# Second LayerNorm of two chunks as a scaling of kept, turned rows, instead of a second turning

## The chip, the cores and the metric

The kernel runs on one core of a Trainium2 chip. The metric is the device time of one execution in microseconds (us). The core has a matrix engine (PE, with its weight loads listed apart as PEld), a vector engine (DVE), a scalar engine (ACT) and GpSimd (POOL); SyncE (SP) issues most DMAs. Each engine works through its own list of instructions in order and waits on semaphores for the others.

## The reference

The input x has 2048 rows of 448 numbers. The kernel computes multi-query attention with 16 heads of width 28 (one head of keys and values for all), and an MLP of width 1792 with a LayerNorm of its own, both on the same normalised rows:

```
xn = layernorm(x)
q = xn @ wq;  k = xn @ wk;  v = xn @ wv
attention = softmax(q k^T / sqrt(28)) v @ wo
y = layernorm(xn)                       # the second LayerNorm
mlp = gelu(y @ w1 + b1) @ w2 + b2
out = x + attention + mlp
```

LayerNorm has no learned scale or shift here. So xn has mean 0, and y is xn times one number for each row: y = a * xn with a = 1 / sqrt(var(xn) + eps).

## The kernel before, in words

The order of the work is written by hand: the kernel states the order of the instructions on each engine, and generators hand out single steps. The 2048 rows are 16 tiles of 128, in four chunks of four tiles (512 rows).

**Precision.** Matrix products that must be exact to float32 are made of three products of halves: each operand is split into a high part (`xh`, rounded to the PE's fp32r type by a copy on ACT) and a low part (`xl`, what is left, by a subtraction on DVE or POOL).

**Turning.** A projection needs the rows with the features on the partitions. `norm_parts` gives two steps for each tile: `center(k)` normalises the tile into `xn` (448 columns on ACT, a last piece of 64 on DVE), and `turn(k)` makes four PE transposes of 128x128 into one PSUM bank, copies the bank to `xh` on ACT (L273) and subtracts `xh` from it on DVE into `xl` (L274). `xh` and `xl` have two buffers each.

**Front** (0 to 67.5 us). For each chunk c there are four slots `q_slot(c, 0..3)`, each a projection of 512 columns by 128 outputs (11 matmuls); their results are evacuated one slot later, by ACT copies and DVE subtractions into `qe`, and stored by SP's queue to DRAM (`qd`), from where the attention loads them by head. Beside chunk c, the next chunk's rows are centered and turned. The fourth chunk has no next one; beside it the first chunk is turned for the second LayerNorm (`second=True`). The strips of w1 are split in the same slots (`w1_split`: ACT copy, two POOL subtractions). `later(c, i, job, ahead)` hangs extra jobs on a slot; `norm_both`, which works out the combined scale `lnq` and shift `lnqb` of both LayerNorms for all 16 tiles, hangs on slots (2, 2) and (2, 3).

**MLP** (67.5 to 475 us). 56 slots: four chunks by 14 strips of 128 hidden units. A slot has the 11 matmuls of the first product (`mlp1`), the 12 of the second (`mlp2`) two slots later, and nine steps for attention in between: row maxima of scores (`max_stream`, L521 and L522) or "turned" scores (`turned_scores`, L555 and L556), which put a fourth head's scores aside in DRAM. The GELU runs on ACT (L603, L604, L609, L616) and POOL (L605, L606, L610, L611, L618). Splitting w2 takes ACT, DVE and POOL in the odd slots of the first 14 (`w2_split`). The chunks go in order 1, 2, 3, 4. In five slots of a chunk (positions 5, 7, 9, 11, 13) `norm_gen` centers and turns a tile of the next chunk for its second LayerNorm; x is loaded again for this by `line(t)`. The first four scores of the MLP and the PSUM tiles of the maxima share one pool of three banks.

**Attention** (475 us to the end). In each step PE makes scores and maxima for one pair of key tiles, ACT takes the exponential, and PE weighs the values. Here the DMAs of the heads are issued by POOL (software DMA), which before are issued by SP.

**Queues.** SP's queue issues in order. A DMA that needs another's data, or a buffer, waits at the head and holds all that stand behind it.

The rows that a chunk needs for its second product are taken in one line of the code before:

```
yh, yl = xts[c, True]
```

Of the kernel before, what the change touches and what calls it, by code (L numbers as in the profile page):

```python
# [9 lines left out]
F32 = mybir.dt.float32  # L10
# [6 lines left out]
P = 128  # L17
# [14 lines left out]
RAWS = 2  # L32
GELU = 0.044715, 0.7978845608028654
LEAD = 11
NH = 8
HD = D // 2

# [2 lines left out]
def block_kernel(ctx, tc, x, wq, wk, wv, wo, w1, b1, w2, b2, out):  # L40
# [20 lines left out]
    ld = dram.tile([4, CW], F32, name="ld")  # L61
    ad = dram.tile([P, NT, D], F32, name="ad")
    td = {u: dram.tile([32, 4, 4 * CT, 512], F32, name=f"td{u}") for u in TURNED}
    qd = [dram.tile([D, S], F32, name=f"qd{i}") for i in range(2)]

    ks = keep.tile([P, S], F32R, name="ks")
# [14 lines left out]
    w1h = wp.tile([P, 4, F], F32R, name="w1h")  # L81
    w1l = wp.tile([P, 3, F], F32R, name="w1l")
    tmp = ph1.enter_context(tc.tile_pool(name="tmp", bufs=2))

    hrp = ph1.enter_context(tc.tile_pool(name="hrp", bufs=3))

# [144 lines left out]
    def norm_both():  # L231
        dve.tensor_mul(lnq, lnp[:, :, 1], lnr)
        dve.tensor_mul(lnq, lnq, lnr)
        r = rstd(lnq, lnq, NT)
        next(r)
        yield
        next(r)
        dve.tensor_mul(lnq, lnq, lnr)
        dve.scalar_tensor_tensor(lnqb, lnp[:, :, 0], -1.0, lnq, op0=ALU.mult, op1=ALU.mult)
        act.activation(warm, one, AF.Tanh)  # L240
        yield

    lines = {}
# [5 lines left out]
    def norm_parts(c, second, first=False, bank=mtile):  # L249
        xh = xt_p.tile([P, 4, CW], F32R, name="xh")  # L250
        xl = xl_p.tile([P, 4, CW], F32R, name="xl")
        xts[c, second] = xh, xl
        xns = {}

        def center(k):
            t = CT * c + k
            if first:
                xn = f(wqp.tile([P, 2, CW], F32R, name="qe", bufs=5))[:, 0, :]
            else:
                xn = tmp.tile([P, 4 * P], F32, name="xn", bufs=2)  # L260
            scale, bias = (lnq, lnqb) if second else (lnr, lnb)
            src = lines.pop(t) if second and c else xin[t]
            act.activation(xn[:, 0:D], src, AF.Identity, bias=bias[:, t:t + 1], scale=scale[:, t:t + 1])
            dve.tensor_scalar(xn[:, D:512], src[:, 384:448], scale[:, t:t + 1], bias[:, t:t + 1],
                              op0=ALU.mult, op1=ALU.add)
            xns[k] = xn

        def turn(k):
            sl = slice(k * P, (k + 1) * P)
            pt = bank([P, 4, P])  # L270
            for b in range(4):
                pe.transpose(pt[:, b, :], xns[k][:, b * P:(b + 1) * P], ident)  # L272
            act.activation(xh[:, :, sl], pt, AF.Copy)  # L273
            dve.tensor_sub(xl[:, :, sl], pt, f(xh[:, :, sl]))  # L274

        return center, turn
# [26 lines left out]
    def norm_gen(c, bank):  # L303
        center, turn = norm_parts(c, True, False, bank)
        for k in range(CT + 1):
            if k > 0:
                turn(k - 1)
            yield
            if k < CT:
                center(k)  # L310
            yield

    wl_q = []

# [98 lines left out]
        for k in range(2):  # L413
            later(c - 1, 0, lambda g=g: next(g), True)
    g = norm_both()
    for k in (2, 3):
        later(2, k, lambda g=g: next(g))

    def b1_turn():
        pb = mtile([P, NF])  # L420
# [23 lines left out]
    turns = itertools.count()  # L444
    evac, vt = None, None
    for c in range(NCH):
        center, turn = norm_parts((c + 1) % NCH, c + 1 == NCH, bank=lambda shape: (qbank, mtile)[next(turns) % 2](shape))
        for i in range(4):
            ev = q_slot(c, i)
            if vt is not None:  # L450
                v_slot(c, vt)
                vt = None
            if evac is not None:
                vt = evac()
            evac = ev
            if i in ((2, 3) if c == 0 else (1, 3)):
                n = 2 * c + i // 3
                w1_split(n)
                if n < 2:
                    w1_load(n + 4)  # L460
                elif n == 3:
                    w1_load2(6)
                elif n in (4, 5):
                    w2_load(n - 4)
                if n in (2, 3):
                    qms.append(load_m(*heads[n - 2]))
                elif n in (4, 5):
                    load_m(TURNED[n - 4], 3, q3[n - 4])
            for job in more.get((c, i, True), ()):
                job()  # L470
            for part, k in (("", "c0 c1", "t0 c2 t1 c3", "t2 t3") if c == 0 else
                            ("c0 c1", "t0 c2 t1 c3", "t2 t3", ""))[i].split():
                (center if part == "c" else turn)(int(k))
            for job in more.get((c, i, False), ()):
                job()
    evac()
    ph1a.close()

    def load_q(u, blocks=range(4)):
# [114 lines left out]
        return c == 0 and ft % 2 == 1  # L594

    def mlp1(c, ft):
        yh, yl = xts[c, True]
        ph = m2p.tile([P, CW], F32, name="m2_3") if (c, ft) == (0, 1) else php.tile([P, CW], F32, name="ph")
        fs = slice(ft * P, (ft + 1) * P)
        yield from proj_steps(ph, lambda b: w1h[:, b, fs], lambda b: w1l[:, b, fs], yh, yl)  # L600
        hx = hrp.tile([P, CW], F32, name="hx", bufs=2)
        hz = hrp.tile([P, CW], F32, name="hz", bufs=2)
        act.activation(hx, ph, AF.Identity, bias=b1t[:, ft:ft + 1])  # L603
        act.activation(hz, ph, AF.Square, bias=b1s[:, ft:ft + 1], scale=GELU[0] ** 0.5)  # L604
        pool.tensor_scalar(hz, hz, 1.0, 1.0, op0=ALU.mult, op1=ALU.add)  # L605
        pool.tensor_mul(hz, hz, hx)  # L606

        def middle():
            act.activation(hz, hz, AF.Tanh, scale=GELU[1])  # L609
            pool.tensor_scalar(hz, hz, 0.5, 0.5, op0=ALU.mult, op1=ALU.add)  # L610
            pool.tensor_mul(hx, hx, hz)  # L611

        def ending():
            hh = hrp.tile([P, CW], F32R, name="hh")
            hl = hrp.tile([P, CW], F32R, name="hl")
            act.activation(hh, hx, AF.Copy)  # L616
            hs[c, ft] = (hh, hl)
            pool.tensor_sub(hl, hx, f(hh))  # L618

        return middle, ending  # L620

    def mlp2(c, ft, stages):
        if ft == 0:
            m2s[c] = [m2p.tile([P, CW], F32, name=f"m2_{k}")[:, 0:D] for k in range(CT)]
        m2 = m2s[c]
        hh, hl = hs.pop((c, ft))
        terms = ((hh, w2h), (hh, w2l), (hl, w2h))
        order = [(k, i) for k in range(CT) for i in range(3)]
        if (c, ft) == (0, 0):
            order.sort(key=lambda e: e[1])  # L630
        for n, (k, i) in enumerate(order):
            h, w = terms[i]
            pe.matmul(m2[k], h[:, k * P:(k + 1) * P], w[:, ft, :], start=(ft == 0 and i == 0),  # L633
                      stop=(ft == NF - 1 and i == 2))
            if ft == NF - 1 and i == 2:
                t = CT * c + k
                a = lines.pop(t)
                dve.tensor_add(a, a, m2[k])
                nc.sync.dma_start(ad[:, t, :], a)
            stages[n]()  # L640
            yield

    def slot(n):
        nonlocal maxed, ending, later_low
        middle = high = low = none
        closing, ending = ending, none
        if n < len(mslots):
            if split(*mslots[n]):
                high, low = w2_split(n // 2)
# [10 lines left out]
            stages, later_low = {0: closing, 1: high, 5: middle}, low  # L660
        if n in norms:
            stages = {4: norms[n], 5: texp, 6: texp, 7: closing, 8: norms[n], 9: middle, 10: low}
        if n >= 2:
            yield from mlp2(*mslots[n - 2], [stages.get(i, none) for i in range(12)])
        else:
            for i in sorted(stages):
                stages[i]()
# [3 lines left out]

    norms, maxed, ending, later_low = {}, 0, none, none
    mslots = [(c, ft) for c in range(NCH) for ft in range(NF)]
    for c in range(1, NCH):
        g = norm_gen(c, lambda shape: php.tile(shape, F32, name="ph"))
        for i in range(CT + 1):
            norms[NF * (c - 1) + 5 + 2 * i] = lambda g=g: next(g, None)
    mxs.add(max_stream())
    done = 0
    for n in range(len(mslots) + 2):  # L680
        c, ft = mslots[n] if n < len(mslots) else (NCH, n - len(mslots))
        if 3 <= ft < 11 and ft % 2 and c < NCH - 1:
            line(CT * (c + 1) + (ft - 3) // 2)
        if 9 < ft:
            line(CT * c + ft - 10)
            if ft > 10:
                a = lines[CT * c + ft - 11]
                pool.tensor_add(a, a, b2b)
        if ft == 0 and n:
            a = lines[CT * c - 1]  # L690
            pool.tensor_add(a, a, b2b)
        if (c, ft) == (NCH - 1, 8):
            load_q(0)
        if (c, ft) == (NCH - 1, 11):
            load_max(0)
        ts = 0
        for _ in slot(n):
            done += 1
            if n >= len(mslots) and done % 3 == 1:
                maxed += mxs.step()  # L700
            elif n < len(mslots) and done * MLP_MAX // 46 > (done - 1) * MLP_MAX // 46:
                if ts < 4 and n < len(mslots) - 1 and not split(c, ft):
                    ts += tq.step()
# [270 lines left out]
```

## Time and profile before

| | us |
|---|---|
| median of 3 runs | 1090.36 (1090.21 to 1091.38) |
| profiled execution | 1091.39 |
| its span in the trace | 1089.6 |
| PE busy | 1077.5 |
| DVE busy | 910.3 |
| ACT busy | 736.8 |
| POOL busy | 561.6 |

The page tells how long each engine was busy in the span, the chain of waits that ended last followed back from the end, and the costliest groups of instructions. The trace also answers for a stretch of time, a line of the code or a tile. A line such as "L618" is a line of the kernel before. The clock that PE was granted was 0.999 of full speed over the span. The last lines of an answer on a tile give the time from a DMA's issue to its landing.

### The profile page before, as it was taken

The numbers are of one execution on the slowest core, as the hardware profiler recorded it, in microseconds if no ns is written. First come the engines' busy times: TensorE is split into PE (matmuls) and PEld (weight loads), VectorE is DVE, ScalarE is ACT, GpSimd is POOL, SyncE is SP. The second block draws the span as 40 slices with busy tenths as digits, with TensorE's granted clock in tenths as the row PEclk, the third lists the DMA queues.
The fourth block names the chain that finished last, engine by engine and source line by source line (L and its number), as shares of the span: only waits on it lengthen the run. The fifth ranks groups of instructions, "written<-read, shape, count | busy, mean of one in ns | idle before, by whom it ended". The sixth has DMA issues, their size and how long they took to land.

```text
span 1089.6 us, 17728 instructions
## 1 busy us (share of the span) xinstructions
PE 1077.5 (99%) x5905; PEld 721.6 (66%) x5905; DVE 910.3 (84%) x1847; ACT 736.8 (68%) x1279; POOL 561.6 (52%) x694
## 2 busy tenths in 40 slices
PE   9999999999999999999999999999999999999998
PEld 8778888888888888865555555555556555455455
DVE  6789889888988998876999997899997889886744
ACT  6775655676666666658777776577775777765784
POOL 5359787768777877864234433433442344243220
PEclk9999999999999999999999999999999999999999
DMA  8774555777877777767987798588796778895720
GB/s 265 221 233 137 154 133 155 193 179 194 211 176 186 187 199 169 219 166 156 197 190 175 184 224 215 131 199 191 182 211 174 176 175 202 193 205 128 189 53 35
DMA packets 140512, 195.16 MB, mean 179 GB/s; under 512 B 17086, under 2 KB 96116, under 8 KB 140420
## 3 DMA queue, kind: packets, MB, share of 16 engines
q1 hardware_dynamic: 127684, 172.11, 63.1%
q0 software_dynamic: 11328, 21.33, 8.7%
q8 instruction: 47, 0.77, 0.3%
q10 hardware_dynamic: 1408, 0.57, 0.2%
q14 instruction: 45, 0.37, 0.1%
HBM read 115.22 MB, written 77.71 MB: 177 GB/s over the span
## 4 chain that ended last, share of the span: by engine, by line
PE 89%; DVE 4%; DMA 3%; ACT 2%; issue 1%; POOL 1%; SPq 0%; DVEq 0%; ACTq 0%; POOLq 0%
PE po L863 20%; PE m L521 18%; PE m L891 17%; PE m L633 11%; PE ph L180 10%; PE m L555 5%; PE m L753 1%; PE m L754 1%; PE m L755 1%; PE ph L185 1%; PE ph L183 1%; PE po L846 1%; DVE xl L274 1%; PE ph L272 1%; DVE mx L522 1%
## 5 line engine op out<-in xcount | busy, mean ns | idle before, releaser
L522 DVE TENSOR_REDUCE mx<-m 128x1 f32<-128x512 f32 x784 | 506.8, 679 | 77.9 <-PE m L521 68.6
L892 ACT ACTIVATE p<-m 128x512 f32<-128x512 f32 x784 | 402.6, 609 | 161.3 <-PE m L891 161.2
L521 PE MATMUL m<-ks,qm 128*128 128x512 f32 x784 | 321.6, 411 | 0.7 <-DVE mx L522 0.6
L891 PE MATMUL m<-xh,ks 128*128 128x512 f32 x784 | 257.2, 397 | 0.1
L863 PE MATMUL po<-p,vs 128*32 128x512 f32 x1920 | 230.8, 598 | 0.0
L521 PEld LDWEIGHTS m<-ks,qm 128*128 128x128 f32 x784 | 147.0, 188 | 117.0 <-ACT p L892 37.0
L891 PEld LDWEIGHTS m<-xh,ks 128*128 128x128 f32 x784 | 146.1, 188 | 42.1 <-issue 5.8
L556 DVE TENSOR_SCALAR_CACHE_REDUCE raw<-m 128x512 f32<-128x512 f32 x240 | 160.9, 689 | 15.3 <-PE m L555 8.6
L874 DVE STREAM_TRANSPOSE p<-half 128x1024 f32<-128x1024 f32 x120 | 148.3, 1236 | 5.3 <-PE m L846 2.0
L573 ACT ACTIVATE raw<-raw,m 128x1024 f32<-128x1024 f32 x120 | 133.0, 1151 | 0.0
L603 ACT ACTIVATE hx<-ph,b1t 128x512 f32<-128x512 f32 x55 | 37.9, 689 | 131.9 <-PE ph L185 124.5
L863 PEld LDWEIGHTS po<-p,vs 128*32 128x32 f32 x1920 | 50.1, 109 | 113.4 <-issue 108.4
L555 PE MATMUL m<-ks,q 128*128 128x512 f32 x240 | 94.8, 395 | 0.9 <-DVE mx L522 0.6
L618 POOL TENSOR_TENSOR hl<-hx,hh 128x512 fp32r<-128x512 f32 x56 | 73.0, 1303 | 35.0 <-ACT hh L616 35.0
L633 PE MATMUL m<-w2h,hl 128*128 128x448 f32 x224 | 82.6, 370 | 1.4 <-POOL hl L618 1.4
L633 PE MATMUL m<-w2l,hh 128*128 128x448 f32 x224 | 81.5, 365 | 0.5 <-DVE w2l L346 0.5
L633 PE MATMUL m<-w2h,hh 128*128 128x448 f32 x224 | 81.4, 364 | 0.0
L611 POOL TENSOR_TENSOR hx<-hx,hz 128x512 f32<-128x512 f32 x56 | 73.0, 1303 | 4.7
L606 POOL TENSOR_TENSOR hz<-hz,hx 128x512 f32<-128x512 f32 x56 | 72.6, 1296 | 4.7
L508 POOL DMA_DIRECT2D xh<-mn x15 | 8.1, 543 | 129.4 <-ACT mn L504 129.3
L180 PE MATMUL ph<-xh,w1h 128*128 128x512 f32 x165 | 65.0, 394 | 0.0
L180 PE MATMUL ph<-xh,w1l 128*128 128x512 f32 x165 | 64.6, 391 | 0.0
(187 smaller groups left out, 1402.3 us busy)
## 6 DMA issues: line engine op xcount, KB each, us to landing
td<-raw SPq DMA_DIRECT2D x240, 256.0 KB
half<-td SPq DMA_DIRECT2D x120, 512.0 KB
xh<-qd POOLq DMA_DIRECT2D x60, 168.0 KB, 4.5
a<-in_A_x_dram SPq DMA_DIRECT2D x32, 224.0 KB
qm<-qd POOLq DMA_DIRECT2D x112, 56.0 KB, 4.3
qd<-qe SPq DMA_DIRECT2D x24, 256.0 KB
qm<-qd SPq DMA_DIRECT2D x84, 56.0 KB
ad<-a SPq DMA_DIRECT2D x16, 224.0 KB
```

The source lines that it names most:

```text
L180: pe.matmul(ps, w, v, start=(n == 0), stop=False)
L521: pe.matmul(pm, qm[:, t * P:(t + 1) * P], ks[:, n * CW:(n + 1) * CW], start=True, stop=True)
L522: dve.tensor_reduce(mx[:, CT * j + t, n:n + 1], pm, axis=AX.X, op=ALU.max)
L555: pe.matmul(sc, q3[i][:, t * P:(t + 1) * P], ks[:, n * CW:(n + 1) * CW], start=True, stop=True)
L556: dve.tensor_scalar(raw[:, :, 4 * n:4 * n + 4, :].rearrange("p r b i -> p b r i"), sc.rearrange("p (b r i) -> p b r i", r=4, i=32), SCALE, ...
L573: act.activation(raw[:, rs], raw[:, rs], AF.Exp, bias=m3[:, 4:5], scale=1.0)
L611: pool.tensor_mul(hx, hx, hz)
L633: pe.matmul(m2[k], h[:, k * P:(k + 1) * P], w[:, ft, :], start=(ft == 0 and i == 0), stop=(ft == NF - 1 and i == 2))
L863: pe.matmul(po[32 * j:32 * j + 32, :], vs[:, kt, :], ps.pop((u, kt, j)), start=(kt == 0), stop=(kt == NT - 1))
L874: dve.transpose(p.rearrange("p k (g j) -> p g k j", j=32), halves[u, kt // 8][:, :, 32 * (kt % 8):32 * (kt % 8) + 64].rearrange("p g (k j) ...
L891: pe.matmul(s, ks[:, kt * P:(kt + 1) * P], qss[u][:, j, :], start=True, stop=True)
L892: act.activation(p, s, AF.Exp, scale=SCALE)
```

## The change

In the front, the rows of chunks 3 and 4 are turned once, for the first LayerNorm, as all chunks are. The change keeps their `xh` and `xl` and scales them in place for the second: row by row by the number a, which for turned rows lies along the free axis.

- `norm_both` moves from slots (2, 2) and (2, 3) to slot (2, 0), and writes the scales a of all tiles to a tile `lna` of its own.
- `scale_rows`, ahead of the turns of slot (2, 1): PE transposes `lna`, DVE copies it, SP stores it to DRAM (`sd`).
- `scale_load`, ahead in slot (2, 2): SP loads a chunk's 512 scales, the same for all partitions, into `ab` (one buffer), chunk 3 first; chunk 4's follow in slot (3, 3).
- For each of the four blocks of features: `join` (DVE adds `xh` and `xl`), `scale` (POOL multiplies by `ab`), `high_part` (ACT copies to `xh`), `low_part` (DVE subtracts to `xl`). For chunk 3 this goes through slots (2, 3) to (3, 2); for chunk 4 through MLP slots 3 to 10, one block in two slots.
- The MLP takes the chunks in the order 3, 4, 1, 2 (`MLP_ORDER`). Only chunks 1 and 2 are turned a second time, beside the second and third position. The front's turning of chunk 1, and its four turns for one chunk in the MLP, are gone, with the loads of four lines of x.
- In MLP slots 3 to 10 one maximum step is left out of each; attention takes those eight.
- The load of the tanh table moves to a job of slot (2, 3).
- `dynamic_dma_scratch_size` is 8192 in place of 16384.

The diff, cut to its core:

```diff
+MLP_ORDER = 2, 3, 0, 1
...
+    sd = dram.tile([NCH, CW], F32, name="sd")
...
+    lna = tmp.tile([P, NT], F32, name="lna", bufs=1)
...
     def norm_both():
         dve.tensor_mul(lnq, lnp[:, :, 1], lnr)
         dve.tensor_mul(lnq, lnq, lnr)
-        r = rstd(lnq, lnq, NT)
+        r = rstd(lna, lnq, NT)
...
-        dve.tensor_mul(lnq, lnq, lnr)
+        dve.tensor_mul(lnq, lna, lnr)
         dve.scalar_tensor_tensor(lnqb, lnp[:, :, 0], -1.0, lnq, op0=ALU.mult, op1=ALU.mult)
-        act.activation(warm, one, AF.Tanh)
...
+    def scale_rows():
+        pa = mtile([NT, P])
+        pe.transpose(pa, lna, ident)
+        at = wqp.tile([NT, P], F32, name="at", bufs=1)
+        dve.tensor_copy(at, pa)
+        nc.sync.dma_start(sd.rearrange("c (k p) -> (c k) p", p=P), at)
+
+    def scale_load(c):
+        scales[c] = tmp.tile([P, CW], F32, name="ab", bufs=1)
+        nc.sync.dma_start(scales[c], sd[c:c + 1, :].to_broadcast([P, CW]))
+
+    def join(c, b):
+        xh, xl = xts[c, False]
+        parts[c, b] = tmp.tile([P, 4 * P], F32, name="xn", bufs=2)
+        dve.tensor_add(parts[c, b], f(xh[:, b, :]), f(xl[:, b, :]))
+
+    def scale(c, b):
+        pool.tensor_mul(parts[c, b], parts[c, b], scales[c])
+
+    def high_part(c, b):
+        act.activation(xts[c, False][0][:, b, :], parts[c, b], AF.Copy)
+
+    def low_part(c, b):
+        xh, xl = xts[c, False]
+        dve.tensor_sub(xl[:, b, :], parts[c, b], f(xh[:, b, :]))
...
-    for k in (2, 3):
-        later(2, k, lambda g=g: next(g))
+    for _ in range(2):
+        later(2, 0, lambda g=g: next(g))
+    later(2, 1, scale_rows, True)
+    later(2, 2, lambda: scale_load(2), True)
+    later(2, 3, lambda: act.activation(warm, one, AF.Tanh))
+    for at, what, bs in (((2, 3), join, (0, 1)), ((3, 0), scale, (0, 1)), ((3, 1), high_part, (0, 1)),
+                         ((3, 1), low_part, (0, 1)), ((3, 1), join, (2, 3)), ((3, 1), scale, (2, 3)),
+                         ((3, 2), high_part, (2, 3)), ((3, 2), low_part, (2, 3))):
+        for b in bs:
+            later(*at, lambda what=what, b=b: what(2, b))
+    later(3, 3, lambda: scale_load(3))
...
+    for c in (2, 3):
+        xts[c, True] = xts[c, False]
...
-        yh, yl = xts[c, True]
+        yh, yl = xts[MLP_ORDER[c], True]
...
+        if n in seconds:
+            scale(3, seconds[n])
...
+        if n in seconds:
+            stages.update({4: lambda: high_part(3, seconds[n]), 6: lambda: low_part(3, seconds[n])})
+        if n + 1 in seconds:
+            stages[8] = lambda: join(3, seconds[n + 1])
...
+    seconds = {4 + 2 * b: b for b in range(4)}
...
-        ts = 0
+        ts, less = 0, n in seconds or n + 1 in seconds
...
+            elif less and done * MLP_MAX // 46 > (done - 1) * MLP_MAX // 46:
+                less = False
...
-    nc = _bacc.Bacc("TRN2", target_bir_lowering=False, num_devices=1)
+    nc = _bacc.Bacc("TRN2", target_bir_lowering=False, num_devices=1, dynamic_dma_scratch_size=8192)
```

More of the change, by code (lines that the diff above doesn't have):

```diff
@@ L261, in center @@
             scale, bias = (lnq, lnqb) if second else (lnr, lnb)
-            src = lines.pop(t) if second and c else xin[t]
+            src = lines.pop(t) if second else xin[t]
             act.activation(xn[:, 0:D], src, AF.Identity, bias=bias[:, t:t + 1], scale=scale[:, t:t + 1])
@@ L311, in norm_gen @@
             yield
+    scales, parts = {}, {}
+    def scale_rows():
[18 more added lines that the diff above has]
+        dve.tensor_sub(xl[:, b, :], parts[c, b], f(xh[:, b, :]))
     wl_q = []
@@ L446, in block_kernel @@
     for c in range(NCH):
-        center, turn = norm_parts((c + 1) % NCH, c + 1 == NCH, bank=lambda shape: (qbank, mtile)[next(turns) % 2](shape))
+        if c + 1 < NCH:
+            center, turn = norm_parts(c + 1, False, bank=lambda shape: (qbank, mtile)[next(turns) % 2](shape))
         for i in range(4):
@@ L471, in block_kernel @@
             for part, k in (("", "c0 c1", "t0 c2 t1 c3", "t2 t3") if c == 0 else
-                            ("c0 c1", "t0 c2 t1 c3", "t2 t3", ""))[i].split():
+                            ("c0 c1", "t0 c2 t1 c3", "t2 t3", "") if c + 1 < NCH else [""] * 4)[i].split():
                 (center if part == "c" else turn)(int(k))
@@ L635, in mlp2 @@
             if ft == NF - 1 and i == 2:
-                t = CT * c + k
+                t = CT * MLP_ORDER[c] + k
                 a = lines.pop(t)
@@ L673, in block_kernel @@
     mslots = [(c, ft) for c in range(NCH) for ft in range(NF)]
-    for c in range(1, NCH):
-        g = norm_gen(c, lambda shape: php.tile(shape, F32, name="ph"))
+    seconds = {4 + 2 * b: b for b in range(4)}
+    for c in range(2, NCH):
+        g = norm_gen(MLP_ORDER[c], lambda shape: php.tile(shape, F32, name="ph"))
         for i in range(CT + 1):
@@ L681, in block_kernel @@
         c, ft = mslots[n] if n < len(mslots) else (NCH, n - len(mslots))
-        if 3 <= ft < 11 and ft % 2 and c < NCH - 1:
-            line(CT * (c + 1) + (ft - 3) // 2)
+        if 3 <= ft < 11 and ft % 2 and 0 < c < NCH - 1:
+            line(CT * MLP_ORDER[c + 1] + (ft - 3) // 2)
         if 9 < ft:
-            line(CT * c + ft - 10)
+            line(CT * MLP_ORDER[c] + ft - 10)
             if ft > 10:
-                a = lines[CT * c + ft - 11]
+                a = lines[CT * MLP_ORDER[c] + ft - 11]
                 pool.tensor_add(a, a, b2b)
         if ft == 0 and n:
-            a = lines[CT * c - 1]
+            a = lines[CT * MLP_ORDER[c - 1] + CT - 1]
             pool.tensor_add(a, a, b2b)
```

## The prediction

> **What bounds the kernel now.** I read the page's totals and the chain that ended last, then the busy time by stretch, then the timelines of the places that the diff touches. From the page:
>
> ```profile
> span 1089.6 us, 17728 instructions
> PE 1077.5 (99%) x5905; PEld 721.6 (66%) x5905; DVE 910.3 (84%) x1847; ACT 736.8 (68%) x1279; POOL 561.6 (52%) x694
> PE 89%; DVE 4%; DMA 3%; ACT 2%; issue 1%; POOL 1%; SPq 0%; DVEq 0%; ACTq 0%; POOLq 0%
> L618 POOL TENSOR_TENSOR hl<-hx,hh 128x512 fp32r<-128x512 f32 x56 | 73.0, 1303 | 35.0 <-ACT hh L616 35.0
> ```
>
> PE works 99% of the span and makes 89% of the chain, so PE time that goes away is gained where nothing else is late. A 128x512 tensor operation on POOL takes 1.30 us. By stretch (start:end, length, then busy us and instruction counts of PE, its weight loads, DVE, ACT, POOL):
>
> ```profile
> 67.50:121.00 53.50, 52.92 (x238) 43.66 (x237) 47.82 (x94) 32.78 (x47) 44.86 (x44) 1.00 0.57 163
> 475.00:1089.00 614.00, 609.16 (x3708) 329.85 (x3706) 497.30 (x912) 437.29 (x845) 216.22 (x344) 1.00 0.74 173
> ```
>
> In the first MLP slots (67.5 to 121 us) PE is full, with DVE (47.8 of 53.5) and POOL (44.9) close behind it. In attention POOL is two thirds idle, PE 99% busy. The span's 1089.6 belongs to an execution of 1091.39; the median of the runs is 1090.36, so I make the sum against 1091.39 and take 1.03 off.
>
> **Turns removed in the front: -2.0 us of PE.** PE's timeline (start, duration, instruction):
>
> ```profile
> 59.85 0.60 PE L272 MATMUL qp<-ident,xn 128*128 128x128 f32 x4
> ...
> 60.64 0.48 PE L180 MATMUL qp<-xh,wah 128*128 128x512 f32 x1
> ...
> 63.70 0.65 PE L272 MATMUL qp<-ident,xn 128*128 128x128 f32 x4
> ...
> 64.89 0.48 PE L180 MATMUL qp<-xh,wah 128*128 128x512 f32 x1
> ...
> 67.50 0.39 PE L180 MATMUL ph<-xh,w1h 128*128 128x512 f32 x1
> ...
> 70.45 0.39 PE L185 MATMUL ph<-xl,w1h 128*128 128x512 f32 x1
> 70.67 0.39 PE L555 MATMUL m<-ks,q 128*128 128x512 f32 x1
> ```
>
> Two turns fill 59.85 to 60.64 and two 63.70 to 64.89: 0.79 + 1.19 = 1.98. With them go their ACT copies and DVE subtractions. The first MLP projection starts at 67.50; its last matmul goes at 70.45, the fourth turned score at 70.67.
>
> **Turns removed in the MLP: -3.9 us.** The GELU input of every slot is read from PSUM by one ACT instruction (L603), so its starts mark the slots:
>
> ```profile
> 108.33 0.69 ACT L603 ACTIVATE hx<-ph,b1t 128x512 f32<-128x512 f32 x1 [3.02 <-PE ph L185]
> 115.36 0.69 ACT L603 ACTIVATE hx<-ph,b1t 128x512 f32<-128x512 f32 x1 [1.81 <-PE ph L185]
> 168.44 0.69 ACT L603 ACTIVATE hx<-ph,b1t 128x512 f32<-128x512 f32 x1 [3.62 <-PE ph L185]
> ```
>
> A slot without a turn takes 115.36 - 108.33 = 7.03. The seven slots after 115.36 hold the four turns made for the second chunk and take 53.08, where 7 x 7.03 = 49.21: 3.87 us for four turns, PE's 0.6 each and waits. In the changed order the rows of chunks 3 and 4 come from kept tiles, so one of three such groups goes. The other two groups only change their chunk.
>
> **Eight maximum scores moved: 0.** Slots 3 to 10 leave out one step each, and attention takes it. A matmul of 128x512 goes every 0.22 to 0.23 us (70.45 to 70.67), so PE gets 8 x 0.23 = 1.8 back in the MLP and pays 1.8 in attention, where it is 99% busy. DVE's 8 reductions have cover there: 497 of 614 us are busy.
>
> **The row of scales: what is late.** Before, the second norm was ready by 57.6 us and only the fourth projection chunk's turns used it. Now it is computed as soon as the last chunk's statistics are in, and the scales must go along the free axis: a PE transpose of `lna`, a DVE copy, a 8 KB store `sd`, a broadcast load `ab` of 256 KB, POOL's product. ACT, DVE and PE around that place and around the second norm of before:
>
> ```profile
> 45.02 1.41 ACT L263 ACTIVATE xn<-hh,lnb,lnr 128x448 f32<-128x448 f32 x2 [1.10 <-DVE lnb L220]
> ```
> ```profile
> 55.96 0.23 ACT L197 ACTIVATE rs<-rs 128x16 f32<-128x16 f32 x1 [1.84 <-DVE rs L195]
> ```
> ```profile
> 53.87 0.17 DVE L232 TENSOR_TENSOR lnq<-lnp,lnr 128x16 f32<-128x16 f32 x1
> ...
> 56.44 0.24 DVE L198 RECIPROCAL rs<-rs 128x16 f32<-128x16 f32 x1
> ...
> 57.36 0.18 DVE L238 TENSOR_TENSOR lnq<-lnq,lnr 128x16 f32<-128x16 f32 x1
> ```
> ```profile
> 45.96 0.60 PE L272 MATMUL qp<-ident,xn 128*128 128x128 f32 x4
> ```
>
> ACT's root stands behind the two centerings (46.43) and takes 0.23; four DVE steps behind it take 57.36 - 56.44 = 0.92, so `lna` is there near 47.6. Its transpose stands on PE ahead of the turn that now starts at 45.96: a stall of some 1.6, and chunk 4's two turns, their copies and the projections behind wait with it. I cost it at nothing, because PE later waits longer for the scaled rows; were that cover gone, it would cost up to 1.6 plus 0.3 for the transpose.
>
> The store and the load go through SP's queue, which runs late in the front. Its issues (start, time for all of a row):
>
> ```profile
> 56.01 1.76 SPq L438 DMA_DIRECT2D q<-qd  x4
> 57.87 2.02 SPq L377 DMA_DIRECT2D qd<-qe  x4
> 59.99 0.86 SPq L334 DMA_DIRECT2D raw<-in_B_w_dram  x1
> ```
>
> In the new order `sd` stands right behind those four `q` loads, so it goes at 57.8 although its data is there some nine microseconds earlier. `ab` stands behind the first two of the `qd` stores and waits for `sd` to land; behind it on SP wait two `qd` stores, the w2 rows and the next `q` loads. In attention the kernel makes the same pair, a small store `ld` and a broadcast load `tr`. Times to landing:
>
> ```profile
> DMA to landing us min/median/max: 1.7/3.8/6.8
> ```
> ```profile
> DMA to landing us min/median/max: 2.1/3.8/5.7
> ```
>
> (first the tile `ld`, then `tr`; `ld`'s answer takes `tr`'s loads in.) So `ab` lands between 57.8 + 1.7 + 2.1 = 61.6 and 57.8 + 6.8 + 5.7 = 70.3; by the medians at 65.4. SP waiting for `sd` also empties the queue, so I take 2.6 and 3.1, below the medians: T = 63.5, an estimate. Everything behind hangs on T. POOL and the two evacuating engines in that place:
>
> ```profile
> 62.24 1.63 POOL L329 TENSOR_TENSOR w1l<-pair,w1h 128x672 fp32r<-128x672 f32 x1 [2.43 <-ACT w1h L328]
> 63.95 0.66 POOL L330 TENSOR_TENSOR w1h<-pair,w1h 64x224 fp32r<-64x224 f32 x1
> ```
> ```profile
> 66.24 0.94 ACT L328 ACTIVATE w1h<-pair 128x896 fp32r<-128x896 f32 x1
> 67.70 0.60 ACT L363 ACTIVATE qe<-qp 128x512 fp32r<-128x512 f32 x1 [0.53 <-PE qp L185]
> ```
> ```profile
> 68.94 0.68 DVE L556 TENSOR_SCALAR_CACHE_REDUCE raw<-m 128x512 f32<-128x512 f32 x1
> ```
>
> POOL's order is two products, the split of the seventh w1 strip (now behind them), two products: 2.6 + 2.4 + 2.6 ends at T + 7.6. The last high part on ACT (0.6) ends near T + 8.2. Behind it ACT has two evacuations of Q and the eighth strip's split: 0.6 + 0.9 + 0.6, T + 10.3; behind that DVE subtracts (0.7, T + 11.0) and only then drains the first turned score (0.7, T + 11.7). There are three PSUM buffers, so the fourth score waits for that drain: 63.5 + 11.7 = 75.2 less some 0.2 for pipelining, 75.0, against 70.67: **+4.3**. It includes the 2.0 that PE gains ahead of it, and the stall. The scaled rows alone would allow the last projection matmuls at T + 8.9 = 72.4, so it is ACT's and DVE's queues that end last.
>
> **POOL and DVE together.** Joins and low parts are DVE operations with two inputs in SBUF. What such company costs:
>
> ```profile
> L346 DVE TENSOR_TENSOR w2l<-raw,w2h x7: 621/1033/1516, 80.0 to 165.2; 128x448 fp32r<-128x448 f32 x7
> ```
>
> The median is 1.03 against 0.62 alone: 0.4 each. In the front two of the four low parts and joins between the products are on the path: +0.8. In slots 3 to 10 POOL gets four products of 1.30 and DVE eight operations, in place of eight reductions; a group of products and halves there has slack, but the first slots have little POOL time left (44.9 of 53.5), so I take +0.5, of 0 to 3.
>
> Removing the reload of four lines takes four DMAs from SP in slots 3 to 9, where nothing waits for it: 0. The table load of tanh moves within the front: 0. Halving the scratch of software DMA concerns POOL's DMAs alone, all in attention, where POOL is idle 398 of 614 us: 0.
>
> The Trainium skill, "SBUF — State Buffer", section "Who interferes with whom", says that a VectorE operation with two SBUF inputs and a GpSimd operation that reads SBUF block each other for a whole instruction. The trace agrees in direction, with 1.03 of median against 0.62. By that rule all four low parts and joins in the front would run one after the other with POOL's work, which is the second rival.
>
> **Sum.** Front +4.3 and +0.8, MLP -3.9 and +0.5, maximum scores -1.8 and +1.8: +1.7. 1091.39 + 1.7 - 1.03 = 1092.0.
>
> **Rivals.** (1) A gain: `ab` lands at the earliest bound, 61.6, nothing collides, and the delay at the fourth score shrinks to 2.4, of which PE's idle time in the first MLP slots (53.50 - 52.92 = 0.58) gives back some 0.5. Then 2.4 - 0.5 - 3.9 = -2.0, and 1088.4; with the first drain no longer behind Q's evacuations another 1 us less, 1087.4. For it speaks that SP's queue has less in front of `ab` than before; against it, that both transfers would have to be at their fastest at once. (2) POOL and DVE strictly one after the other: four operations of 0.65 between the products put 2.6 on the path in place of 0.8: +3.5, and 1093.8. For it speaks L346's longest, 1.52; against it, that its shortest is 0.62. (3) `ab` lands by the medians, 65.4: +1.9, and 1093.9; with (2), 1095.7. (4) The smaller scratch makes POOL's queue in attention wait for landings. It decides from the point where POOL's 398 idle us are used up; that nothing in the trace shows such a wait leaves it unpriced and outside the range.
>
> **How the numbers follow.** My forecast has 0.45 (1089.6 to 1093.6 by itself), rival 1 0.2, rivals 2 and 3 0.3, the rest 0.05. A change of 0.2%, 2.2 us, is about what a measurement can tell here: faster means below 1088.2, slower above 1092.5. Rival 1 gives 0.16 faster and 0.04 same; the forecast 0.02 faster, 0.3 same and 0.13 slower; the rest 0.35 slower. That is 0.18, 0.34 and 0.48. The range goes from rival 1's 1087.3 to rivals 2 and 3 together, 1096.0.
>
> **What would show it.** Right: `sd` issued near 57.8 and `ab` landing at 63 to 64; POOL's first product right behind it; the fourth turned score near 75; no turn in the MLP's first 14 slots (each 7.03 from the fifth on). Wrong: products before 60 us, or PE without a stall near 70; a slot among 3 to 10 longer than 7.1; the attention stretch longer by more than 1.8.

## The result and the profile after

The changed kernel takes 1103.93 us (median of 4 runs, 1103.37 to 1105.37) against 1090.28: a ratio of 1.0125, with a 95% interval of 1.0107 to 1.0143. That is 13.6 us slower, where 1.7 was forecast. The profiled execution took 1103.37 and spans 1101.6, 12.0 more than before.

The page of the changed kernel, its first totals and the chain that ended last:

```profile
span 1101.6 us, 17647 instructions
PE 1077.4 (98%) x5874; PEld 719.8 (65%) x5874; DVE 917.6 (83%) x1848; ACT 733.1 (67%) x1271; POOL 577.7 (52%) x706
PE 87%; DVE 5%; ACT 3%; DMA 2%; POOL 1%; issue 1%; SPq 0%; ACTq 0%; POOLq 0%; DVEq 0%
```

PE has 31 instructions fewer and the same busy time, 1077.4 against 1077.5, so in sum the others took longer. The chain has more of DVE and ACT (4% and 2% before). I divide the span at five marks of the trace: the fourth turned score, the start of the GELU input (L603, now L645) in the slots with numbers 3 and 14, counted from 0, the first attention score, and the end. All are starts in us.

| profiled execution | 4th score | slot 3 | slot 14 | attention | end | attention lasts |
|---|---|---|---|---|---|---|
| before | 70.67 | 86.95 | 168.44 | 475.51 | 1089.6 | 614.1 |
| changed | 77.36 | 95.92 | 175.92 | 482.13 | 1101.6 | 619.4 |
| difference | +6.7 | +9.0 | +7.5 | +6.6 | +12.0 | +5.3 |

So there are three places: the front and the first MLP slots lose 9.0, the slots from 3 to 14, which were to win some 5, win 1.5 (and the slots from 14 on 0.9, of which nothing was forecast), and attention, which was to pay 1.8, pays 5.3. A mark moves by itself too: e12 below has the front of the kernel before, word for word, and its fourth score and slot 3 come 0.8 earlier.

**The front.** SP's and POOL's timelines of the changed kernel (start, duration, instruction, and in brackets the idle time before it and what ended it):

```profile
57.09 0.31 SPq L322 DMA_DIRECT2D sd<-at  x1
...
59.91 0.32 SPq L326 DMA_DIRECT2D ab<-sd  x1
```
```profile
64.18 2.52 POOL L334 TENSOR_TENSOR xn<-xn,ab 128x512 f32<-128x512 f32 x2 [7.34 <-DMA ab<-sd]
...
70.71 2.79 POOL L334 TENSOR_TENSOR xn<-xn,ab 128x512 f32<-128x512 f32 x2 [0.72 <-DVE xn L331]
```

The scales arrive just ahead of 64.18, after 7.34 us in which POOL did nothing. The second pair of products waits 0.72 for the joins, which stand on DVE behind the low parts. DVE's and PE's timelines:

```profile
66.17 3.30 DVE L341 TENSOR_TENSOR xl<-xn,xh 128x512 fp32r<-128x512 f32 x2 [6.21 <-ACT xh L337]
```
```profile
70.09 0.40 PE L597 MATMUL m<-ks,q 128*128 128x512 f32 x1
72.98 0.49 PE L183 MATMUL ph<-xh,w1h 128*128 128x512 f32 x1 [2.49 <-ACT xh L337]
74.10 0.79 PE L183 MATMUL ph<-xl,w1h 128*128 128x512 f32 x1 [0.63 <-DVE xl L341]
...
77.36 0.79 PE L597 MATMUL m<-ks,q 128*128 128x512 f32 x1 [0.75 <-DVE raw L598]
```

Two low parts take 3.30, although the shortest of the tile takes 0.69; POOL is at work nearly throughout beside them. And from 74.10 on PE's matmuls are long: 0.79 and 0.63 in place of 0.39. The busy times by stretch, with the granted PE clock third from the end of a row, tell why:

```profile
72.00:74.00 2.00, 0.49 (x1) 0.19 (x1) 1.34 (x2) 1.10 (x2) 1.50 (x2) 1.00 0.34 131
74.00:76.00 2.00, 1.90 (x5) 1.49 (x5) 1.34 (x3) 1.97 (x4) 0.44 (x1) 0.51 0.24 94
78.00:80.00 2.00, 2.00 (x6) 1.60 (x5) 1.82 (x6) 0.64 (x1) 1.85 (x2) 0.50 0.84 283
82.00:84.00 2.00, 2.00 (x10) 1.65 (x10) 1.78 (x4) 1.10 (x3) 1.76 (x2) 1.00 0.54 120
```

PE, busy for 0.98 of the 4 us from 70 to 74, is granted half its clock from 74 until after 80.

**The MLP slots with chunk 4's scaling.** DVE, POOL, ACT and PE in slot 4 of the changed kernel:

```profile
106.25 1.69 DVE L341 TENSOR_TENSOR xl<-xn,xh 128x512 fp32r<-128x512 f32 x1 [0.99 <-ACT xh L337]
```
```profile
106.10 1.29 POOL L648 TENSOR_TENSOR hz<-hz,hx 128x512 f32<-128x512 f32 x1
```
```profile
105.60 0.62 ACT L337 ACTIVATE xh<-xn 128x512 fp32r<-128x512 f32 x1
```
```profile
108.59 0.50 PE L563 MATMUL m<-ks,qm 128*128 128x512 f32 x1 [0.54 <-DVE mx L564]
```

DVE stands 0.99 us until ACT has made the high part (106.22), then is blocked by POOL's product until 107.39; its operation takes 1.69. The maxima behind it drain late, and PE, with its three banks full, waits. PE's waits between 84 and 175 us, first of the kernel before, then of the changed one (its second row is the w2 split of the first slots; columns are us in total, times, longest):

```profile
PE m L555 <- DVE mx L522: 0.6, 3, 0.2
```
```profile
PE m L563 <- DVE mx L564: 3.2, 4, 1.3
PE m L675 <- DVE w2l L376: 1.3, 1, 1.3
```

Four waits of 3.2 in all as the profile counts them. By the distance from one PE instruction to the next they cost some 0.17 more each, 3.9. The seven slots from number 7 take 175.92 - 124.90 = 51.0, where 7 x 7.03 less the three steps left out among them (0.23 each) is 48.5.

**Attention.** PE has two waits near the end that the kernel before has not. First the kernel before at the same transpose, then the changed kernel:

```profile
1032.77 0.96 PE L891 MATMUL m<-xh,ks 128*128 128x512 f32 x3
1033.57 0.27 PE L501 MATMUL m<-ident,mr 128*12 128x128 f32 x1
```
```profile
1042.24 0.39 PE L563 MATMUL m<-ks,qm 128*128 128x512 f32 x1
1043.78 0.27 PE L543 MATMUL m<-ident,mr 128*12 128x128 f32 x1 [1.15 <-DVE mr L568]
...
1060.66 0.64 PE L897 MATMUL m<-p,vs 128*32 128x256 f32 x8 [1.56 <-ACT p L943]
```

The first is the transpose of the last unit's maxima, which now stands right behind the last three of them on PE; in the kernel before the step had scores alone ahead of it. The second comes 17 us later, at the start of the last unit's value product, and ends when ACT has made the last of six exponentials (1057.57 + 3.04 = 1060.61):

```profile
1057.57 3.04 ACT L943 ACTIVATE p<-m 128x512 f32<-128x512 f32 x6
```

The kernel's text gives a reason for it: in attention the PSUM tiles are handed out in a ring of seven banks, and the last unit's value product takes one certain bank of them (`mp1`) for its second half. Eight tiles more move the ring on by one place, and then the last score before that product can be what sits in this bank. The trace does not name banks, so this is read from the code and not shown.

### The profile page after: what moved, and what is told of

It is laid out like the page before. It is cut to its first block, busy times and chain, and to the rows that moved or that the text cites. A ratio compares the mean times of both kernels' runs of the same rounds, so it can differ in the third digit from the quotient of the medians.

```text
span 1101.6 us, 17647 instructions
## 1 busy us (share of the span) xinstructions
PE 1077.4 (98%) x5874; PEld 719.8 (65%) x5874; DVE 917.6 (83%) x1848; ACT 733.1 (67%) x1271; POOL 577.7 (52%) x706
## 4 chain that ended last, share of the span: by engine, by line
PE 87%; DVE 5%; ACT 3%; DMA 2%; POOL 1%; issue 1%; SPq 0%; ACTq 0%; POOLq 0%; DVEq 0%
PE po L914 20%; PE m L563 17%; PE m L942 17%; PE m L675 10%; PE ph L183 9%; PE m L597 5%; PE m L804 1%; PE m L805 1%; PE m L806 1%; DMA qd<-qe 1%; PE ph L186 1%; PE ph L188 1%; ACT raw L615 1%; PE qp L183 1%; DVE xl L341 1%
## 5 line engine op out<-in xcount | busy, mean ns | idle before, releaser
L645 ACT ACTIVATE hx<-ph,b1t 128x512 f32<-128x512 f32 x55 | 37.8, 688 | 125.0 <-PE ph L188 124.4
L477 POOL DMA_DIRECT2D qm<-qd x116 | 59.3, 522 | 17.6 <-PE m L942 13.9
L183 PE MATMUL ph<-xl,w1h 128*128 128x512 f32 x165 | 65.4, 396 | 2.3 <-DVE xl L341 1.6
```

What stands on the lines that cost most here:

```text
L183: pe.matmul(ps, w, v, start=(n == 0), stop=False)
```

## The experiments

Theory A was that the loss has these three places with these causes: the row of scales comes late by SP's queue, and PE, idle, then runs at half its clock; DVE, standing at the low parts, holds PE up; and the eight maxima moved into attention put the last ones in the way of the work that needs them. The kernel before was run beside each group of runs; its medians were 1090.3 to 1090.8. The marks of the profiled executions in one table, the edits below:

| kernel | median | 4th score | slot 3 | slot 14 | attention | attention lasts |
|---|---|---|---|---|---|---|
| before | 1090.3 | 70.67 | 86.95 | 168.44 | 475.51 | 614.1 |
| changed | 1103.9 | 77.36 | 95.92 | 175.92 | 482.13 | 619.4 |
| e1, maxima kept | 1107.5 | 75.25 | 94.69 | 182.29 | 488.64 | 614.4 |
| e10, PE kept busy | 1102.1 | 77.20 | 93.49 | 174.23 | 480.25 | 619.6 |
| e4, scale row by PE | 1095.7 | 70.06 | 86.80 | 167.59 | 474.15 | 619.2 |
| e5, MLP half alone | 1095.1 | 70.18 | 86.49 | 167.30 | 473.57 | 619.3 |
| e6, e4 and maxima later | 1091.4 | 70.44 | 87.17 | 167.97 | 476.06 | 613.6 |
| e7, e4 and low parts later | 1093.5 | 70.85 | 87.57 | 166.14 | 472.53 | 619.1 |
| e11, e4 with both | 1090.6 | 70.95 | 87.64 | 166.11 | 475.20 | 613.7 |
| e9, e5 with both | 1089.5 | 70.28 | 86.58 | 165.04 | 473.96 | 613.6 |
| e13, e9, low parts later still | 1088.7 | 70.03 | 86.31 | 164.12 | 473.46 | 613.6 |
| e12, before with half the scratch | 1090.4 | 69.89 | 86.17 | 167.65 | 474.48 | 614.3 |

**e1: the maxima stay in the MLP.**

```diff
-        ts, less = 0, n in seconds or n + 1 in seconds
+        ts, less = 0, False
```

> The changed kernel (1103.9), but MLP slots 3 to 10 keep all nine steps, so attention gets no maxima back. Theory A (the attention stretch grew by 5.4 us because of the eight maximum steps: 1.8 of matmuls, and some 3 in two waits near its end, where the last maxima now stand right ahead of the transpose that needs them): attention is as long as in the kernel before, within 0.7; the MLP slots pay 1.8 and up to 2 more where DVE is full; 1100 to 1102. Theory B (attention grew for another reason, such as the smaller scratch): attention stays 5 us longer, and the time goes up to 1105 to 1107.

Measured: 1107.5 (two runs, 1104.8 and 1110.2; the marks are those of the faster). Attention lasts 614.4, as in the kernel before (614.1): its 5.3 came from the eight steps. In the MLP I was wrong about the price: slots 3 to 14 take 87.6 in place of 80.0, 7.6 more, where 3.8 at most was expected. With the ninth step PE's waits for DVE more than double, and the granted clock is 0.93 over 25 us in the middle of these slots, so a part of the 7.6 is the clock's. PE's waits between 84 and 175 us, to be held against those of the changed kernel above, and the stretch with the lower clock:

```profile
PE m L563 <- DVE mx L564: 7.8, 4, 2.2
PE m L675 <- DVE w2l L376: 1.3, 1, 1.3
```
```profile
125.00:150.00 25.00, 22.67 (x95) 18.97 (x96) 21.42 (x39) 10.68 (x16) 17.41 (x16) 0.93 0.39 103
```

So leaving the steps out was a relief for those slots; giving them to attention was the error.

**e3 and e8: idle matmuls, twice in the wrong place.**

```diff
+        if (c, ft) == (0, 0):
+            filler = m2p.tile([P, CW], F32, name="m2_0")[:, 0:P]
+            before = lambda b: spin((8, 8, 20)[b], filler)
```

In e8 the tile was the third of that pool. `before` runs ahead of each of the three blocks of the first projection.

> The changed kernel with 36 idle 128x128 matmuls on PE in the first MLP slot, ahead of the first matmul of each of three blocks, where PE waits for the scaled rows. The wait for the data stays. Theory A (the idle PE was granted half its clock from 74 to 81 us, which costs 13 matmuls 0.2 us each): clock 1.00 throughout, 2 to 3 us faster, 1101 to 1102. Theory C (PE's clock there does not matter, since ACT, DVE and POOL are what is late): within 0.7 of 1103.9.

> The changed kernel (1103.9) with the 36 idle matmuls in the first MLP slot as in e3_busy_pe, now into a PSUM bank that the front gives free early, so that they hold nothing up. Theory A (half the clock from 74 to 81 us costs 13 matmuls 0.2 us each): clock 1.00 from 66 to 84, 2 to 3 us faster, 1101 to 1102. Theory C (PE's clock there does not matter): within 0.7 of 1103.9.

Measured: 1114.1 and 1114.3. The bank was one of Q's, and the idle matmuls waited for the last evacuation (PE of e8):

```profile
76.64 3.78 PE L431 MATMUL m<-ident 128*128 128x128 f32 x16 [10.58 <-DVE qe L402]
```

They say nothing on the theories, except that the clock is half after 10.6 us of idle: 16 of these matmuls took 3.78, the next 16 took 2.20. From the first of them to the last long matmul it was four microseconds in e3 and over five in e8.

**e10: idle matmuls that wait for nothing.** The tile is the next of the pool of three banks, and 35 matmuls are spread over the first projection's five waits:

```diff
+            filler = mtile([P, P])
+            before = lambda n: spin({0: 6, 1: 5, 4: 8, 6: 12, 7: 4}.get(n, 0), filler)
```

> The changed kernel (1103.9) with 35 idle matmuls in the first MLP slot, spread over the five places where PE waits for scaled rows, into a PSUM bank that PE itself freed, so that they wait for nothing. Theory A (half the clock from 74 to 81 us costs 13 matmuls 0.2 us each, 2.7): PE busy nearly throughout from 66 to 74, clock 1.00, 2 to 3 us faster than the changed kernel, 1101 to 1102. Theory C (PE's clock does not matter there): within 0.7 of 1103.9.

Measured: 1102.1 (two runs, 1101.6 and 1102.6; the changed kernel's four are 1103.4 to 1105.4), 1.8 less than the changed kernel. The stretches of e10:

```profile
70.00:74.00 4.00, 4.00 (x35) 3.88 (x34) 3.10 (x6) 2.29 (x4) 2.30 (x2) 1.00 0.64 197
74.00:78.00 4.00, 3.62 (x22) 2.97 (x22) 3.25 (x9) 1.38 (x4) 2.28 (x2) 1.00 0.82 269
78.00:82.00 4.00, 4.00 (x20) 3.30 (x19) 3.65 (x8) 3.89 (x7) 2.34 (x3) 1.00 0.15 58
```

The clock stays whole. The fourth score comes no earlier (77.20), since its data are as late, but slot 3 does, by 2.4, and the start of attention by 1.9. The halved clock thus costs about 2 of the front's 9, a little less than the 2.7 that I had counted from the matmuls. The Trainium skill, "TensorE: Matmul & The Clock Gate", section "HAM oscillation — how this bites in real kernels", tells the same mechanism: a PE that waits too long is throttled to half its clock, and the work behind the wait starts slow. The trace agrees, with 0.50 from 76 to 80 us and 1.00 where PE was kept busy. The section's rule speaks of idle gaps above some 3.4 us; here no wait was over 2.49, so for this trace the rule is too narrow.

**e4: the row of scales without the DMAs.**

```diff
     def scale_load(c):
-        scales[c] = tmp.tile([P, CW], F32, name="ab", bufs=1)
-        nc.sync.dma_start(scales[c], sd[c:c + 1, :].to_broadcast([P, CW]))
+        pa = mtile([P, CT, P])
+        for k in range(CT):
+            t = CT * c + k
+            pe.matmul(pa[:, k, :], lna[:, t:t + 1].to_broadcast([P, P]), ident, start=True, stop=True)
+        scales[c] = tmp.tile([P, CW], F32, name="ab", bufs=1)
+        dve.tensor_copy(scales[c].rearrange("p (k j) -> p k j", k=CT), pa)
```

`scale_rows` is empty here.

> The changed kernel, with the row of scales made by four PE matmuls of a broadcast column with the identity into one PSUM bank and one DVE copy to SBUF, in place of the transpose, the store and the broadcast load. Theory A (the trip through SP's queue, which ended at 64.0, makes the front late): the scale row is there before 56, the fourth turned score at 69 to 71 in place of 77.4, the clock stays at 1.00, and 6 to 9 us go: 1095 to 1098. Theory D (POOL and DVE blocking each other is the front's main cost): the score comes at 73 to 75, 1099 to 1102.

Measured: 1095.7, 8.2 less. DVE and POOL of e4:

```profile
51.72 0.68 DVE L326 COPY ab<-m 128x512 f32<-128x512 f32 x1
```
```profile
56.21 2.88 POOL L334 TENSOR_TENSOR xn<-xn,ab 128x512 f32<-128x512 f32 x2
```

The row is there at 52.4 in place of 64, the products start at 56.2, and the fourth score comes at 70.06, 7.3 earlier. The trip through SP's queue made the front late. e4 also takes away a wait of PE for `lna` ahead of the transpose, 1.26 in the changed kernel, and no run parts the two. What POOL and DVE cost each other did not go (two joins take 2.57 here), but is hidden then. Slot 3 is level with the kernel before (86.80 against 86.95): the four turns taken out of the front and the scaling put in are worth the same, 0 in place of -2. Over all runs it is rather a loss: in the four kernels with this front (e4, e6, e7, e11) slot 3 starts at 86.80 to 87.64, in the five with the front of before (before, e5, e9, e12, e13) at 86.17 to 86.95, and in the medians e4 is 0.6 above e5 and e11 1.1 above e9. The trace shows where a part of it goes. The first MLP projection starts at 65.71 in e4 and at 67.50 before, but the fourth score comes 4.35 behind that, where it was 3.17; 0.57 of it is a wait for DVE's copy of chunk 4's row:

```profile
68.84 0.51 PE L597 MATMUL m<-ks,q 128*128 128x512 f32 x1 [0.57 <-DVE ab L326]
```

**e5: the MLP half alone.** Front as before; chunk 1 is turned there for the second norm, and chunk 4 alone is scaled:

```diff
-MLP_ORDER = 2, 3, 0, 1
+MLP_ORDER = 0, 3, 1, 2
...
+    later(3, 2, scale_rows)
+    later(3, 3, lambda: scale_load(3))
...
-    for c in (2, 3):
-        xts[c, True] = xts[c, False]
+    xts[3, True] = xts[3, False]
```

> The MLP half of the change alone: the front is that of the kernel before (with the turning of the first chunk and the old places of the second norm), the scale row is made late in the front and used for chunk 4 only; order 1, 4, 2, 3; one maximum step left out in slots 3 to 10 as in the changed kernel. Theory A (the MLP half gains 3.9 by the turns and 1.8 by the steps left out, loses 3.9 in four waits for DVE, and attention is 4.6 longer): the first slots as before within 0.7, slots 3 to 10 alternately near 7.7 and 6.8, 1092.5 to 1094.5. Theory E (the waits in slots 3 to 10 come from the late front): those slots take 6.8 each, and 1088.5 to 1090.5.

Measured: 1095.1, 0.6 above the range that A gave. Slots 3 to 14 take 80.8, as in the changed kernel (80.0) and in e4 (80.8), without any late front, so theory E falls: those waits are the MLP half's own. Attention is 5.2 longer again. The front half of the change is what lies between this kernel and the changed one: 8.8 us.

**e6: the maxima done later in the MLP.** Eight slots of the last chunk take one step more:

```diff
+            elif extra and done % 23 > 17 and done * MLP_MAX // 46 == (done - 1) * MLP_MAX // 46:
+                maxed += mxs.step()
+                extra = False
```

with `extra` set for slots 44 to 51.

> The kernel with the scale row made on PE (1095.7), and with the eight maximum steps that slots 3 to 10 leave out done in slots 44 to 51, one more in each, so that attention gets as many as in the kernel before. Theory A (eight more maxima put the last ones right ahead of the work that needs them, which costs 2 to 3 us in waits near the end, beside 1.8 of matmuls that only change place): attention as long as before within 0.5, the MLP 1.8 longer, 1092.5 to 1093.8. Theory F (the waits near the end have another cause, such as where steps fall against DMAs): 1095 to 1096.

Measured: 1091.4, 4.3 less than e4 and 1.1 below the range that A gave. Attention lasts 613.6 and PE's two waits are gone; the MLP pays 1.9 (attention starts at 476.06 in place of 474.15). Attention is 5.6 shorter (613.6 against 619.2). If the eight matmuls cost 1.9 here too, as in the MLP, some 3.6 are left. The two waits are 2.7 of this as the profile counts them.

**e7: the low parts later.**

```diff
-            stages.update({4: lambda: high_part(3, seconds[n]), 6: lambda: low_part(3, seconds[n])})
+            stages.update({4: lambda: high_part(3, seconds[n]), 9: lambda: low_part(3, seconds[n])})
```

> The kernel with the scale row made on PE (1095.7), and with chunk 4's low parts on DVE three PE steps later in their slots (tenth step of the second product in place of the seventh). Theory A (DVE stands at the low part, 1 us for the high part of ACT and 1 us for POOL, and PE then waits for a drained bank): the first of the two goes, the four waits of PE shrink from 0.8 to 1.5 us to 0.3 or less, 1092.5 to 1094. Theory G (DVE is full in these slots, wherever the low part stands): the waits only move, 1095 to 1096.5.

Measured: 1093.5, 2.3 less than e4, in A's range, though the longest wait is 0.6 and not 0.3. PE's waits for DVE between 84 and 175 us go from 4.0 (e4) to this:

```profile
PE m L563 <- DVE mx L564: 1.5, 4, 0.6
```

**e11, e9 and e13: the causes taken away together.** e11 is e4, and e9 is e5, each with the low parts as in e7, two steps left out in slots 4, 6, 8, 10 and one in 3, 5, 7, 9, and these twelve done one each in slots 42 to 53. e13 is e9 with the low parts at step 11.

> The kernel with the scale row made on PE, chunk 4's low parts three steps later, two maximum steps left out in each of the slots 4, 6, 8, 10 and one in 3, 5, 7, 9, and the twelve done one each in slots 42 to 53. If the three causes add up as they were measured (4.3 for the maxima, 2.3 for the low parts, and a rest of four waits of 0.3 to 0.8): 1088 to 1089.5. If they cover each other: 1090.5 to 1091.5.

> The MLP half alone (front of the kernel before; 1095.1), with the low parts later and the twelve maximum steps of slots 3 to 10 done in slots 42 to 53. Adding up: 1087.5 to 1089. If the causes cover each other: 1090 to 1091.5.

> As e9_half_tuned (1089.5), with chunk 4's low parts two PE steps later still, at the last step of their slots. DVE then has maxima to drain while POOL's product and ACT's high part end, in place of 0.94 us idle at 96.6; POOL's next product still blocks the low part. Theory A (that idle time of DVE is what PE still waits for in slots 5 to 11): PE's four waits of 0.5 to 1.0 go to 0.3 or less, 1087.5 to 1088.7. Theory G (DVE is full there): 1089.2 to 1090.

Measured: e11 1090.6, ratio to before 0.9996 (0.9987 to 1.0006), so no difference. From e4 it is 5.1 less, where the parts had 4.3 and 2.3, so they cover each other by 1.5. e9 1089.5, 0.999 (0.9981 to 0.9999), between its two ranges. e13 1088.7, 0.9981 (0.9972 to 0.999), at the upper end of A's range: 0.2% faster than the kernel before. PE's waits in e13 between 84 and 175 us:

```profile
PE m L555 <- DVE mx L556: 1.5, 5, 0.3
```

None is over 0.3 any more, though the low part itself still takes 1.80 or 1.81 beside POOL's product. Slots 3 to 14 take 77.8, against 81.5 in the kernel before; a part of the 3.7 are steps of maxima that slots 42 on take over. The seven slots from number 7 hold 42 matmuls for maxima in place of 47 and take 49.8 in place of 53.1 (starts 114.31 to 164.12): 1.1 of the 3.3 are those five steps, so 2.1 of the 3.9 of the four turns are kept here.

**e12: half the scratch in the kernel before.**

```diff
-    nc = _bacc.Bacc("TRN2", target_bir_lowering=False, num_devices=1)
+    nc = _bacc.Bacc("TRN2", target_bir_lowering=False, num_devices=1, dynamic_dma_scratch_size=8192)
```

> The kernel before with the halved DMA scratch (8192) alone. Theory A (it costs nothing): 1090.2 to 1091.6, attention as long as before. Theory B (POOL's queue waits for room): attention longer by 1 us or more, above 1092.

Measured: 1090.4 beside 1090.7, ratio 0.9997 (0.9986 to 1.0007); attention lasts 614.3 against 614.1. The scratch costs nothing. The reverse (e2), the changed kernel with the old scratch, gave no time, since it does not fit the memory.

## Why the prediction was wrong

**When the scales arrive: right.** T was put at 63.5; POOL's first product starts at 64.18. The store went at 57.09 (57.8 forecast). So was the cause: e4 takes the trip away and 8.2 us go.

**What follows T: mis-sized by 0.9.** The fourth score was to come at 75.0, or 75.8 with the collisions, which is 11.5 or 12.3 after T; it came at 77.36, 13.2 after 64.18. The step that failed is "two of the four low parts and joins between the products are on the path: +0.8"; the runs show 1.7 in its place. The second products started at 70.71, where T + 5.0 would be 69.2. Half of these 1.5 is the wait for the joins, since the first two low parts alone took 3.30, 1.9 more than two of 0.69. The other half is POOL's own: the split of the strip took 2.7 in place of 2.4, and a small operation of 0.54 (`b1s`), which the order had left out, stands ahead of it. The second rival, one after the other, had 2.6 for this, too much by as much as 0.8 was too little. Its condition held for the first two low parts, not for all four operations.

**The idle PE: left out.** I costed the stall as waiting alone: the wait was reckoned to end at 75.0 and work to go on at 0.23 a matmul. From 74 to 81 the matmuls went at half the clock. The sum had no term for this, and e10 puts it at 1.8 in the time and 2.4 at slot 3. The other stall, at the transpose of `lna`, was put at some 1.6 and costed at nothing; it took 1.26, PE did wait for the scaled rows later, and no run shows it by itself.

**The MLP's turns: mostly lost again.** PE's turns did go, 3.9 by the kernel before. But of this the seven slots keep 53.1 - 51.0 - 0.7 (three steps left out) = 1.4 in the changed kernel, and 2.1 in e13. The step "a group of products and halves there has slack ... I take +0.5, of 0 to 3" failed: PE lost 3.9 in the four waits, outside its own bounds, and slots 3 to 14 won 1.5 where 3.9 of turns and 1.8 of steps left out were to be had. I looked at POOL's slack, and what PE waited for was DVE: a low part holds it for 0.99 of waiting and 1.0 of being blocked, with its reductions behind it and PE behind those. Moving the low part (e7) gave 2.3 back without any less work. What keeps the rest of the turns' gain away can be read from the traces. In the seven slots from number 7 PE has two of the waits in the changed kernel, which cost 2.5 by the distance between PE instructions, and three short ones in e13, which cost 1.6: about what is missing of 3.9. In e13 POOL is busy for 48.6 of these 49.8 us, so there would have been little more to win.

**The eight maxima: "0" was wrong by 3.5 to 4.** The matmuls did only change place (e6: 1.9 in the MLP). But the last maxima fell into the step whose transpose needs them, and PE waited 1.15 there. It waited another 1.56 at the last unit's value product. This wait too is in all five kernels with eight more and in none with the old count; that it comes from the ring of banks, and not from the place of the maxima, is argued from the code. e1 and e6 show it from two sides: with the old count attention lasts 614.4 and 613.6, with eight more 619.1 to 619.6 in five kernels. DVE's cover of 497 of 614 us was no argument, for what counts is what stands around the last maxima, not the share over the stage.

**The rest.** Halving the scratch at 0 was right (e12). The four front turns, -2.0, were right as PE time, but what replaces them eats them, and by e4 against e5 and e11 against e9 some 0.6 to 1.1 more, even when the row is not late.

In sum, 1.7 was forecast and 12.0 came by the spans. Missing were 3.9 in the front up to slot 3 (9.0 against 5.1), 3.7 in slots 3 to 14 (a gain of 1.5 against 5.2) and 3.5 in attention (5.3 against 1.8); the slots from 14 on gave 0.9 that was not forecast. The first 3.9 are 0.7 of T, 0.9 of what follows it, and 2.3 from the fourth score to slot 3, where the clock is.

## What to carry to other kernels

Before taking work off the busiest engine, look at what stands in order on the next one: an operation that waits on a third engine holds up every drain behind it, and here moving it three steps was worth 2.3 us. Work that is moved "at the same price" needs its last piece placed: ask what consumes it, and how many steps later. A small row of numbers that has to turn from partitions to the free axis was better made on PE here than sent through a queue that runs late.

## What the hardware showed that was not expected

PE fell to half its clock although its longest single wait, as the profile counts it, was 2.49 us; in the eight microseconds from 66 to 74 it had been busy for 3.16. It was back at full clock some six to seven microseconds after its work went on. And a DVE subtraction with two inputs in SBUF took 1.69 us instead of 0.69 when POOL's 1.29 us product had started 0.15 us ahead of it: the whole of the rest of that product (1.14) and then its own time, less some overlap. All four low parts in the MLP slots start within 0.15 us behind such a product and take 1.69 to 1.82; in e4 one with nothing on POOL beside it takes 0.69.
